# Strassen's seven products in the first feed-forward product of four chunks, on one Trainium2 core

## The chip, the core and the metric

The kernel runs on one core of a Trainium2 chip. The metric is the device time of one execution in microseconds. Before the change four runs gave 675.12, 676.35, 673.66 and 674.65 us; the median is 674.89. The core's engines have their own instruction queues and wait for each other by semaphores: PE multiplies matrices into PSUM, and its weight loads are listed apart as PEld; DVE (vector), ACT (scalar) and POOL (GpSimd) do elementwise work; SP issues most transfers. [...]

## What is computed

A linear attention (delta rule) over 4 batches, 8 heads, 768 tokens and head size 48 is followed by a feed-forward network with a leaky slope for each feature, on 3072 tokens:

```python
for t in range(S):
    kt, vt, bt = (k_n[:, :, t], v[:, :, t], beta[:, :, t, None])
    y[:, :, t] = np.einsum('bhd,bhde->bhe', q[:, :, t], state)
    v_old = np.einsum('bhde,bhd->bhe', state, kt)
    state = state + bt[:, :, :, None] * np.einsum('bhd,bhe->bhde', kt, vt - v_old)
...
h = x @ w_in                                  # 3072 x 384 by 384 x 2048
g = np.maximum(h, 0.0) + alpha * np.minimum(h, 0.0)
return (g @ w_out).astype(np.float32)         # 3072 x 2048 by 2048 x 384
```

Everything is float32. `x` is `y` with its heads side by side.

## The kernel before, in words

**Chunks and steps.** The sequence is cut into 12 chunks of 64 tokens. A chunk of all four batches has 256 tokens. The attention treats two batches at a time, so there are 24 steps `n`, two for each chunk, and every step depends on the state that the step two before it left. When both steps of a chunk `c` are done, `to_ffn` has transposed the chunk's output into `xts[c]`, three blocks of 128 model dimensions by 256 tokens, and the feed-forward of that chunk can run.

**First product, `ffn_in` (L894).** Features are taken in pairs of 128. For each pair, six matmuls (two feature blocks, three blocks of the contraction) of 256 columns fill one PSUM bank `p_ffn` (L903). ACT then takes Relu of the negated bank (L913), and DVE, once for each block of features, multiplies by the slope and adds the bank (L915). The result lies in `act`. There are eight pairs in a chunk. Two banks take turns.

**Second product, `ffn_out_fast` (L955).** From chunk 2 on this product already uses Strassen's scheme (Winograd's form): seven products of 192 columns, each over the eight pairs (L967), instead of eight. It needs sums of blocks of `act`, made by DVE in `operand_sums` (L848, L857), four for each half of the pairs, and sums of the weights, made once. DVE adds the seven products up (L987), and the rows are stored.

**The order of the work** is written out by hand; instructions stand on each engine's queue in program order. From step `JOINED` on, each step has three bursts of attention on PE: `burst_a` (L1070: the outputs and the next state of the step before, the reading of the state for this one), `turn_round` (L1101: transposes) and `burst_b` (L1090: the solve, Gram matrices, and two small products). Between them `stretch` (L1403) deals out a number of parts of the feed-forward, and with `weave` shares other pieces among them: elimination pieces on DVE (`blocks`), copies on ACT that place blocks (`placing`, L615) and what the burst returned as `later`. The feed-forward lags the attention by about one chunk; that of chunk 11 runs after the attention has ended.

**PSUM** has eight banks. Six are three pairs `p_big`, taken in turn by the bursts; two are the `p_ffn` banks.

**Names that the steps below touch:** the query is the product of `q` with the state in `through_state` (L735 to L739), copied to `y` by ACT (L755). `k_t` has nine rotating buffers, `same` and `block` one each (elimination), `k_early` three for keys that have been loaded ahead. The last elimination is that of steps 20 to 23.

Of the kernel before, what the change touches and what calls it, by code (L numbers as in the profile page):

```python
# [32 lines left out]
C = 64  # L33
# [2 lines left out]
BUSY = 8  # L36
EARLY = 8
FIRST = 6


@with_exitstack
def kernel(
# [26 lines left out]
    work = ctx.enter_context(tc.tile_pool(name="work", bufs=2))  # L69
    psum = ctx.enter_context(tc.tile_pool(name="psum", bufs=1, space=bass.MemoryType.PSUM))  # L70

    def ps_big():


        return psum.tile([128, 2, 512], FP32, name="p_big", tag="big", bufs=3)

    def ps_one():
        return ps_big()[:, 0]

    ffn_banks = [psum.tile([128, 512], FP32, name=f"p_ffn{i}") for i in range(2)]  # L80
    turn = [0]

    def ps_ffn():
# [3 lines left out]
    def half(i):  # L87
        return slice(64 * i, 64 * i + 64)

    def dims(i):  # L90
        return slice(64 * i, 64 * i + D)
# [224 lines left out]
    def by_parity(x):  # L316
        return x.rearrange("p (g a) d -> p a g d", a=2)
# [70 lines left out]
    def quarters():  # L388
        return [(g, a, t) for g in range(G) for a in range(2) for t in range(2)]

    def now(pieces):
        for x in pieces:
            x()

    def region(p, n, **into):

        p = ps_big()[:, :, 0:n] if p is None else p
        assert p.shape[-1] == n
        return p.rearrange("p a (g i) -> p a g i", **into)
# [310 lines left out]
        return [filled]  # L710


    nv, rhs_, ys, us, xts = {}, {}, {}, {}, {}

    def scale_v(n):
        if n < N and n not in nv:
            nv[n] = v_raw.pop(n)
            nc.vector.tensor_tensor(
                out=nv[n], in0=nv[n],
                in1=stats[n][0][:, :, None].to_broadcast([128, H, D]), op=ALU.mult,  # L720
            )

    def through_state(n, p=None, p_y=None):
        if n >= N:
            return []
        c, bp = steps[n]
        if c == 0:
            rhs_[n] = by_parity(nv[n])
            return []
        p = region(p, G * (D + C), g=G)  # L730
        for g, a, t in quarters():
            nc.tensor.matmul(  # L732
                p[half(t ^ a), a, g], k_t[n][dims(a), g, half(t)], beside[bp][dims(a), t, g]
            )
        p_y = region(p_y, G * D, g=G)  # L735
        for g, a, t in quarters():
            nc.tensor.matmul(  # L737
                p_y[half(t), a, g], q_t[n][dims(a), t, g], state[bp][dims(a), t, g]
            )  # L739

        r = work.tile([128, 2, G, D], FP32, name="r")
        v_in = by_parity(nv[n])
        y = work.tile([128, H, D], FP32, name="y")
        rhs_[n], ys[n] = r, y

        def less(to, own, a):
            nc.vector.tensor_tensor(  # L747
                out=r[to, a], in0=v_in[to, a], in1=p[own, a, :, 0:D], op=ALU.subtract
            )

        return [
            lambda: less(slice(0, 128), slice(0, 128), 0),
            lambda: less(half(0), half(1), 1),
            lambda: less(half(1), half(0), 1),
            lambda: nc.scalar.copy(by_parity(y), p_y),  # L755
            lambda: masked(n, p[:, :, :, D : D + C]),
        ]

# [48 lines left out]
    def to_ffn(n, p=None):  # L807
        c, bp = steps[n]
        if bp == 0:
            xts[c] = work.tile([128, KT, TOK], FP32, name="xt", tag="xt", bufs=NXT)  # L810
        p = (ps_one() if p is None else p)[:, 0:DM]
        y = ys[n].rearrange("p h d -> p (h d)")
        for t in range(KT):
            nc.tensor.transpose(p[:, t * 128 : (t + 1) * 128], y[:, t * 128 : (t + 1) * 128], ident)  # L814

        nc.scalar.copy(  # L816
            xts[c].rearrange("p k (u b t i) -> p b k u t i", u=2, b=NB, t=2)[:, bp],
            p.rearrange("p (k t u i) -> p k u t i", k=KT, t=2, u=2),
        )


    gss = {}
# [132 lines left out]
    def ffn_out_fast(c):  # L955
# [58 lines left out]
        store(c, 1, o[1])  # L1014
        yield

    in_done, out_done = [], []
    IN_PARTS, OUT_PARTS, FAST_PARTS = FT * KT, NB * FT, 7 * FP // 2


    def part(gen, n):
        for _ in range(n):
            next(gen, None)
            yield
# [45 lines left out]
    def burst_a(n):  # L1070

        soon, later = [], []
        b = ps_big()
        if n > JOINED:
            soon += outputs(n - 1, b[:, :, 0:WY])
            soon += next_state(n - 1, b[:, :, WY : 2 * WY])
            later.append(lambda: load_late(n + 1))
        if n < N:
            p, y = ps_big(), ps_big()
            soon += through_state(n, p[:, :, 0 : G * (D + C)], y[:, :, 0:WY])  # L1080
            if n < JOINED + 2:
                soon += between_1(n + 1, b[:, :, 2 * WY : 2 * WY + G * HB])
            if n == JOINED:
                soon += grams(n + EARLY, y[:, :, WY : WY + G * C])
                later.append(lambda: squares(n + EARLY + 1))
            later.append(lambda: load_v(n + 3))
        now(soon)
        return later

    def burst_b(n):  # L1090

        b, x = ps_big(), ps_big()[:, :, 0 : G * C]
        soon = solve(n, b[:, :, 0:WY])
        gram = grams(n + EARLY + 1, x)
        soon += between_2(n + 1, b[:, :, WY : WY + G * HB])
        if n > JOINED:
            soon += between_1(n + 2, b[:, :, 2 * WY : 2 * WY + G * HB])
        now(soon + gram[:2])
        return gram[2:] + [lambda: squares(n + EARLY + 2)]

    def turn_round(n):  # L1101
# [24 lines left out]

    def queries():

        p = [x.rearrange("p (n g i) -> p n g i", n=2, g=G) for x in ffn_banks]
        for n in range(2):  # L1130
            for g, a, t in quarters():
                nc.tensor.matmul(
                    p[a][half(t ^ a), n, g], k_t[n][dims(a), g, half(t)],
                    q_t[n][dims(a), t, g],
                )
            a_t[n] = work.tile([128, H, C], FP32, name="a_t")

        def mask(n):
            for a in range(2):
                nc.vector.tensor_tensor(  # L1140
                    out=a_t[n][:, a * G : (a + 1) * G], in0=p[a][:, n],
                    in1=minus[:, None, :].to_broadcast([128, G, C]), op=ALU.mult,
                )

        return mask
# [248 lines left out]
    weave((prelude(NJ), 4), (catch_up(), 2 * (EARLY - FIRST)), (part(late, few), few))  # L1394

    def feed_forward():
        for c in range(2, NCH):
            yield from ffn_in(c)
            yield from ffn_out_fast(c)

    tail = feed_forward()

    def stretch(n, blocks, share, later, *gens):  # L1403

        gens = [(*x, 0.0) for x in (*gens, (part(tail, n), n))]
        gens += [(part(blocks, share), share, 0.3), (each(later), len(later), 0.5)]
        weave(*[x for x in gens if x[1] > 0])

    blocks, share = eliminate(2), WHOLE // 3
# [9 lines left out]
    TURNS = [(3, 3, 4), (3, 3, 4), (4, 4, 4), (0, 5, 6)]  # L1419
    FILL = {JOINED: (8, 12, 12), JOINED + 1: (10, 12, 10), JOINED + 2: (8, 10, 12)}  # L1420
    FILLS = [(12, 10, 12), (12, 18, 12)]
    for n in range(JOINED, N):
        fill, share = FILL.get(n, FILLS[n % 2]), PIECES_OF.get(n, TURNS[n % NJ])
        extra = [[], [], []]
        if n == JOINED:
            place(n + 1, (0,))
            extra[1] = [(weight_sums(1, 0, 3), 3)]
            extra[2] = [(weight_sums(0, 3, 4), 1)]
        elif n == JOINED + 1:
            extra[0] = [(weight_sums(1, 3, 4), 1), (placing(n + 1, (1, 2, 3)), PLACING)]  # L1430

        later = burst_a(n)
        stretch(fill[0], blocks, share[0], later, *extra[0])
        later = turn_round(n)
        if n == JOINED:
            extra[1].append((placing(n + 1, (1, 2, 3)), PLACING))
        stretch(fill[1], blocks, share[1], later, *extra[1])
        m, ends = (n + 6) // NJ, n % NJ == 2
        if ends and n > JOINED:
            for _ in blocks:  # L1440
                assert False
            place(n + 2, (0,))
        later = burst_b(n) + [lambda: scale_v(n + 1)]
        if n == JOINED:
            stretch(fill[2], blocks, share[2], later, *extra[2])
            for _ in blocks:
                assert False
            place(n + 2, (0,))
            place(n + 3, (0,))
            blocks = eliminate(m)  # L1450
        else:
            if ends:
                blocks = eliminate(m) if m < N // NJ else iter(())
            after = [(placing(n + 2, (1, 2, 3)), PLACING)]
            if n % NJ != 1:
                after.append((placing(n + 3, (0,)), 1))
            stretch(fill[2], blocks, share[2], later, *after, *extra[2])
    stretch(12, iter(()), 0, burst_a(N))
    to_ffn(N - 1)
    for _ in tail:  # L1460
# [31 lines left out]
```

## Time and profile before

The profiled execution took 675.12 us; its span, from the first to the last instruction, is 673.4 us.

| what | us | share of the span |
|---|---|---|
| PE busy | 651.0 | 97% |
| PE, first product (L903), 1152 records | 261.6 | |
| DVE busy | 452.4 | 67% |
| ACT busy | 271.0 | 40% |
| POOL busy | 35.7 | 5% |
| first product of chunk 8 starts at | 489.74 | |
| first product of chunk 9 starts at | 538.36 | |
| first product of chunk 10 starts at | 586.17 | |
| first product of chunk 11 starts at | 630.60 | |
| second product of chunk 11 starts at | 651.32 | |

The page cuts the span into 40 slices and gives each engine's busy share in tenths:

```profile
PE   6999999999998999999999999999999999999997
...
DVE  4956879868989869748959748759655355354261
ACT  4927755336565353353353353243244144020110
POOL 6000121001010000001000000000000000000000
```

Each digit is one slice of 16.8 us, 9 being 90% or more. A float32 matmul is listed as two records with a weight load each, so the 48 matmuls of one chunk's first product are 96 records. [...]

### The profile page before, as it was taken

How to read it: one execution, taken by the hardware profiler on the slowest of the kernel's cores; microseconds unless marked ns; L12 is line 12 of the kernel's file. 1: busy time of each engine (PE TensorE's matmuls, PEld its weight loads, DVE VectorE, ACT ScalarE, POOL GpSimd, SP SyncE). 2: the span in 40 equal slices, each digit the busy share in tenths (PEclk: the TensorE clock that was granted, in tenths of full speed). 3: DMA queues.
4: the chain of work that ended last, by engine and by line, in shares of the span. 5: the costliest groups of instructions: out<-in, count | busy, mean ns of one | idle time of the engine just before them, and what ended most of it. 6: DMA issues, size and time to landing. Idle time of an engine off the chain costs nothing.

```text
span 673.4 us, 21591 instructions
## 1 busy us (share of the span) xinstructions
PE 651.0 (97%) x9359; PEld 567.4 (84%) x9359; DVE 452.4 (67%) x1125; ACT 271.0 (40%) x643; POOL 35.7 (5%) x105
## 2 busy tenths in 40 slices
PE   6999999999998999999999999999999999999997
PEld 5578877666687998998998998988989989989997
DVE  4956879868989869748959748759655355354261
ACT  4927755336565353353353353243244144020110
POOL 6000121001010000001000000000000000000000
PEclk9979999999999999999999999999999999999999
DMA  8837844211432022122112111111111110100000
GB/s 130 235 94 209 208 107 118 71 37 30 80 61 49 17 58 48 25 50 49 25 38 37 26 37 37 26 42 31 28 44 27 37 37 2 37 1 2 23 1 24
DMA packets 110959, 37.69 MB, mean 56 GB/s; under 512 B 104160, under 2 KB 107248, under 8 KB 110864
## 3 DMA queue, kind: packets, MB, share of 16 engines
q1 hardware_dynamic: 109088, 35.81, 24.3%
q8 instruction: 74, 1.21, 0.7%
q10 hardware_dynamic: 1776, 0.49, 0.4%
q14 instruction: 21, 0.17, 0.1%
HBM read 31.56 MB, written 4.72 MB: 54 GB/s over the span
## 4 chain that ended last, share of the span: by engine, by line
PE 77%; DVE 14%; ACT 6%; issue 2%; DMA 1%; ACTq 0%; POOL 0%; SPq 0%; DVEq 0%; POOLq 0%
PE p_ffn L903 30%; PE p_ffn L967 28%; DVE prod L499 2%; PE p_big L360 2%; DVE block L505 2%; PE p_big L762 2%; PE p_big L732 2%; PE p_big L775 2%; PE p_big L407 2%; DVE act L915 2%; PE p_big L1121 2%; ACT diag L631 1%; PE p_big L737 1%; PE p_big L791 1%; DMA ke<-in_k_dram 1%
## 5 line engine op out<-in xcount | busy, mean ns | idle before, releaser
L903 PE MATMUL p_ffn<-xt,w_in 128*128 128x256 f32 x1152 | 261.6, 382 | 6.0 <-ACT act L913 1.8
L903 PEld LDWEIGHTS p_ffn<-xt,w_in 128*128 128x128 f32 x1152 | 214.4, 190 | 37.7 <-issue 3.1
L915 DVE SCALAR_TENSOR_TENSOR act<-act,al_t,p_ffn 128x256 f32<-128x256 f32 x176 | 76.6, 477 | 79.6 <-ACT act L913 79.5
L913 ACT ACTIVATE act<-p_ffn 128x512 f32<-128x512 f32 x88 | 52.4, 595 | 143.0 <-PE p_ffn L903 142.7
L967 PE MATMUL p_ffn<-w_out,act 128*128 128x192 f32 x480 | 82.5, 328 | 0.2 <-DVE act L915 0.2
L967 PEld LDWEIGHTS p_ffn<-w_out,act 128*128 128x128 f32 x480 | 77.6, 190 | 1.0 <-issue 0.5
L505 DVE TENSOR_TENSOR block<-block,prod 128x30 f32<-128x30 f32 (+9 forms) x150 | 49.9, 333 | 5.1
L499 DVE TENSOR_TENSOR prod<-block 128x30 f32<-128x30 f32 (+9 forms) x150 | 48.9, 326 | 3.3 <-POOL block L489 1.6
L987 DVE TENSOR_TENSOR o_sb<-u,p_ffn 128x192 f32<-128x192 f32 x40 | 13.3, 352 | 50.3 <-PE p_ffn L967 41.9
L816 ACT COPY xt<-p_big 128x384 f32<-128x384 f32 x22 | 10.4, 477 | 74.2 <-PE p_big L814 74.2
L967 PE MATMUL p_ffn<-space_out,sums 128*128 128x192 f32 x160 | 29.4, 327 | 0.0
L967 PE MATMUL p_ffn<-more,sums 128*128 128x192 f32 x160 | 29.3, 326 | 0.0
L755 ACT COPY y<-p_big 128x384 f32<-128x384 f32 x22 | 10.4, 476 | 43.0 <-PE p_big L737 41.4
L967 PE MATMUL p_ffn<-w_out,sums 128*128 128x192 f32 x160 | 27.6, 326 | 0.0
L967 PEld LDWEIGHTS p_ffn<-more,sums 128*128 128x128 f32 x160 | 26.6, 190 | 0.0
L967 PEld LDWEIGHTS p_ffn<-space_out,sums 128*128 128x128 f32 x160 | 26.5, 190 | 0.1
L967 PEld LDWEIGHTS p_ffn<-w_out,sums 128*128 128x128 f32 x160 | 26.3, 190 | 0.0
L708 ACT COPY inv<-p_big 32x256 f32<-32x256 f32 x38 | 13.8, 362 | 29.7 <-DVE u L766 29.4
L631 ACT ACTIVATE diag<-inverse,which 64x128 f32<-64x128 f32 (+2 forms) x60 | 24.3, 405 | 2.4 <-DVE inverse L472 1.4
L747 DVE TENSOR_TENSOR r<-v_raw,p_big 64x192 f32<-64x192 f32 (+1 forms) x66 | 23.2, 352 | 1.0
L332 DVE TENSOR_REDUCE norm<-ksq 128x8 f32<-128x384 f32 x24 | 13.0, 545 | 13.5 <-ACT ksq L330 13.5
L349 POOL TENSOR_TENSOR beta_t<-beta_t,rec 128x8 f32<-128x8 f32 x24 | 6.2, 260 | 291.6 <-DVE rec L347 271.3
(161 smaller groups left out, 954.2 us busy)
## 6 DMA issues: line engine op xcount, KB each, us to landing
w_out<-in_moe_w_in_dram SPq DMA_DIRECT2D x12, 512.0 KB, 5.6
qp<-in_q_dram SPq DMA_DIRECT2D x48, 96.0 KB, 3.0
v_raw<-in_v_dram SPq DMA_DIRECT2D x48, 96.0 KB, 2.8
kl<-in_k_dram SPq DMA_DIRECT2D x96, 48.0 KB, 2.5
out_dram<-o_sb SPq DMA_DIRECT2D x92, 48.0 KB, 1.6
space_out<-in_moe_w_out_dram SPq DMA_DIRECT2D x11, 384.0 KB, 3.9
ke<-in_k_dram SPq DMA_DIRECT2D x43, 96.0 KB, 3.1
w_out<-in_moe_w_out_dram SPq DMA_DIRECT2D x5, 384.0 KB, 4.6
```

The lines of the kernel that those rows point to most:

```text
L360: nc.tensor.transpose(p[0:ROWS, g * 128 : (g + 1) * 128], src[:, 2 * g : 2 * g + 2].rearrange("p h d -> p (h d)")[:, 0:ROWS], ident,)
L407: nc.tensor.matmul(p[half(t), a, g], k_t[n][dims(a), g, half(t)], k_t[n][dims(a), g, half(t)])
L499: nc.vector.tensor_tensor(out=prod, in0=r[:, 0:j, j : j + 1].to_broadcast([128, j, n]), in1=r[:, j : j + 1, j + 1 : HB].to_broadcast([128, ...
L505: nc.vector.tensor_tensor(out=r[:, 0:j, j + 1 : HB], in0=r[:, 0:j, j + 1 : HB], in1=prod, op=ALU.add)
L631: nc.scalar.mul(out, x, which[rows, i : i + 1])
L708: nc.scalar.copy(to[rows], p[rows])
L732: nc.tensor.matmul(p[half(t ^ a), a, g], k_t[n][dims(a), g, half(t)], beside[bp][dims(a), t, g])
L747: nc.vector.tensor_tensor(out=r[to, a], in0=v_in[to, a], in1=p[own, a, :, 0:D], op=ALU.subtract)
L903: nc.tensor.matmul(p_h[:, i], w_in[:, t, (f + i) * 128 : (f + i + 1) * 128], xt[:, t], start=(t == 0), stop=(t == KT - 1),)
L913: nc.scalar.activation(g, p_h, ACT.Relu, scale=-1.0)
L915: nc.vector.scalar_tensor_tensor(out=g[:, i], in0=g[:, i], scalar=al_t[:, f + i : f + i + 1], in1=p_h[:, i], op0=ALU.mult, op1=ALU.add,)
L967: nc.tensor.matmul(p, x(i), w(i), start=(i == 0), stop=(i == FP - 1))
```

## The change

In chunks 8 to 11 (`FAST_IN = 8`) the first product of each feature pair is made anew. The first two blocks of the contraction, the two blocks of features and the two halves of the tokens make two-by-two blocks of 128; they are multiplied by Strassen's seven products (Winograd's form) of 128 columns. The third block of the contraction stays as it was: two matmuls of 256 columns into the same bank. So a pair has 2 matmuls of 256 columns and 7 of 128, instead of 6 of 256.

Three of the seven products go straight into the pair's bank; four go into a bank of their own (`shared`), which ACT copies to SBUF; POOL forms three running sums there, and DVE adds the result to the pair's bank (`total`). Relu (`below`) and slope then work on SBUF. `Due` puts these pieces at counted places later in the order: the total one pair on, Relu and slope two pairs on, except for the last pairs. Relu has two buffers, and the last total and slope are put ahead of most operand sums.

The sums of the weights (`input_sums`, eight on DVE) are made once, beside the second product of chunk 7; they lie in `same`, in buffers of early keys, in a `k_t` buffer and, in place, in `w_in`. The sums of the tokens (`token_sums`, four on DVE) are made for each chunk during the second product of the chunk before.

From step 16 on PSUM is divided into two pairs for the attention instead of three, and four banks for the feed-forward. The query moves from `burst_a` of a step to `burst_b` of the step before. Copies that `burst_b` left for later are shared out from an earlier point (`soon=0.1`), and `placing` is put off to the stretch after the next `burst_a`. In chunks 8 to 11 `ffn_out_faster` replaces `ffn_out_fast`: the same seven products in another order, with the last two pairs of the first two products held back, and the store of the second half of the rows first.

```diff
-        return psum.tile([128, 2, 512], FP32, name="p_big", tag="big", bufs=3)
+        big.append(big.pop(0))
+        return big[-1]
...
+    banks(3, 0)
...
+    def query(n, p=None):
...
+        for g, a, t in quarters():
+            nc.tensor.matmul(
+                p[half(t), a, g], q_t[n][dims(a), t, g], state[bp][dims(a), t, g]
+            )
+        ys[n] = work.tile([128, H, D], FP32, name="y")
+        return [lambda: nc.scalar.copy(by_parity(ys[n]), p)]
...
+            for dst, x, y, op in (
+                (s1, a21, a22, ALU.add), (s2, s1, a11, ALU.subtract),
+                (s3, a11, a21, ALU.subtract), (a21, a12, s2, ALU.subtract),
+            ):
+                nc.vector.tensor_tensor(out=dst, in0=x, in1=y, op=op)
+                yield
...
+        for dst, a, b in (
+            (0, x(0, 1), x(0, 0)), (1, x(1, 1), t[:, 0]), (2, x(1, 1), x(0, 1)),
+            (3, x(1, 0), t[:, 1]),
+        ):
+            nc.vector.tensor_tensor(out=t[:, dst], in0=a, in1=b, op=ALU.subtract)
...
+    def ffn_in_fast(c):
...
+            p = ffn_banks[i % 3]
+            q = quarter(ffn_banks[2 if i == 0 else 3])
...
+            def own():
+                whole(0)
+                yield
+                more(0, w(1, 0), x(1, 0))
+                more(1, w(0, 1), x(1, 1))
+                yield
+                whole(1)
+                yield
+                more(2, w(1, 1), t[:, 3])
+                yield
+
+            def common():
+                shared(0, w(0, 0), x(0, 0))
+                shared(1, s(1), t[:, 1])
+                yield
+                shared(2, s(2), t[:, 2])
+                shared(3, s(0), t[:, 0])
+                nc.scalar.copy(z, q)
+                for dst, a, b in (
+                    (z[:, 1], z[:, 0], z[:, 1]), (z[:, 2], z[:, 1], z[:, 2]),
+                    (z[:, 1::2], z[:, 1:3], z[:, 3:4].to_broadcast([128, 2, 128])),
+                ):
+                    nc.gpsimd.tensor_tensor(out=dst, in0=a, in1=b, op=ALU.add)
+                yield
+
+            def total():
...
+                nc.vector.tensor_tensor(
+                    out=h, in0=p, in1=z.rearrange("p i e -> p (i e)"), op=ALU.add
+                )
+
+            def below():
...
+                nc.scalar.activation(r.rearrange("p f i -> p (f i)"), h, ACT.Relu, scale=-1.0)
+
+            def slope():
+                for f in range(2):
+                    nc.vector.scalar_tensor_tensor(
+                        out=g[:, f], in0=r[:, f], scalar=al_t[:, 2 * i + f : 2 * i + f + 1],
+                        in1=g[:, f], op0=ALU.mult, op1=ALU.add,
+                    )
+
+            due.put(PER * (i + 1) + {0: PER, FP - 1: 2}.get(i, 3), total)
+            due.put(PER * (i + 2) + {FP - 2: 1, FP - 1: -4}.get(i, 2), below)
+            due.put(PER * (i + 2) + {FP - 2: 1, FP - 1: -2}.get(i, 5), slope)
+            for gen in (own(), common()) if i == 0 else (common(), own()):
+                for _ in gen:
+                    due.step()
+                    yield
...
+    def ffn_out_faster(c):
...
+        yield from some(*a, range(FP - 2))
+        yield from some(*b, range(FP - 2))
+        yield from some(*a, range(FP - 2, FP))
+        nc.scalar.copy(u[0], p[0])
+        yield from some(*b, range(FP - 2, FP))
+        add(o[0][:, left], u[0], p[1])
+        yield from some(p[2], operand(1, 1), w_sum_(3), range(FP))
...
+        asked = query(n + 1, x[:, :, 0:WY]) if n + 1 >= LATE else []
...
+        if n >= LATE:
+            now(soon[:1])
+            return soon[1:] + asked
...
+        if n == LATE:
+            banks(2, 2)
...
-        stretch(fill[0], blocks, share[0], later, *extra[0])
+        stretch(fill[0], blocks, share[0], later, *extra[0], *put_off)
```

## The prediction

> **What bounds the kernel now.** I read the page's first part, then sums over windows, then waits, then the timeline.
>
> ```profile
> PE 651.0 (97%) x9359; PEld 567.4 (84%) x9359; DVE 452.4 (67%) x1125; ACT 271.0 (40%) x643; POOL 35.7 (5%) x105
> ```
>
> PE is busy for 97% of the span, but an average hides stages. The changed stretch runs from the feed-forward of chunk 8 (489.74 us) to the last matmul. Three of its windows (chunk 8 with two attention steps; first product of chunk 11; its second product):
>
> ```profile
> 489.74:538.36 48.62, 48.40 (x672) 44.37 (x671) 24.54 (x52) 17.02 (x40) 0.00 (x0) 1.00 0.17 34
> 630.60:651.32 20.72, 20.72 (x98) 18.24 (x97) 8.96 (x19) 4.18 (x7) 0.00 (x0) 1.00 0.04 12
> 651.32:669.50 18.18, 18.18 (x113) 18.07 (x111) 5.49 (x12) 0.92 (x2) 0.00 (x0) 1.00 0.05 12
> ```
>
> The columns are length, then busy PE, PEld, DVE, ACT, POOL, then clock. PE has no gap, DVE is half used, POOL is empty, the clock is full. The waits of PE from 488 us to the end agree:
>
> ```profile
> PE p_big L665 <- ACT diag L631: 0.2, 1, 0.2
> ```
>
> So every PE nanosecond removed here shortens the run, as long as the new ACT, POOL and DVE work keeps up. After the last matmul an addition (0.35) and the store take 4 us; both versions end so.
>
> **PE, removed and added.** An f32 matmul leaves two records. The first product of chunk 11 is 96 records in 20.72 us: 215.8 ns each at 256 columns. One pair of feature blocks has 12 records, 2.590 us. Afterwards it has 4 records of 256 columns and 14 of 128 (seven 128-column products). What does a 128-column record cost, each with its own weight load?
>
> ```profile
> 555.21 0.49 PE L814 MATMUL p_big<-ident,y 128*128 128x128 f32 x3
> 555.53 0.60 PE L360 MATMUL p_big<-ident,qp 128*112 128x128 f32 x4
> 555.97 0.38 PE L903 MATMUL p_ffn<-xt,w_in 128*128 128x256 f32 x1
> ...
> 555.86 0.30 PEld L903 LDWEIGHTS p_ffn<-xt,w_in 128*128 128x128 f32 x2
> ```
>
> From 555.21 to 555.97 stand seven records: 109 ns each. These are transposes, with a weight load of 140 ns on the PEld side where the product's takes 190. But the first load for L903 begins at 555.86 and its matmul at 555.97: the load of the very shape in question, begun with the transpose before, holds nothing up within one 109 ns slot. At 36.1 us one ordinary f32 matmul of 128 columns (L1121) shows 109 ns between its two records too, with a 190 ns load between.
>
> [...] The row has single f32 loads only, never a long stream; still it shows the load of this very shape inside the slot, so I take 109.2. Break-even is 109.2 + 198/14 = 123.3 ns. Below nothing there is no end: fewer columns can't gain more than their share.
>
> Four chunks of eight pairs: 32 x 0.198 = **6.3 us** removed. Going from 128 to 256 columns costs 3 ns (the record after 555.97 came after 219 instead of 216), twice a pair: 0.2 back.
>
> **New work beside PE, per pair of 2.39 us.** ACT: a PSUM copy of 128x512 (nearest row: L381, 112x512, 582 ns) and Relu from SBUF (L913, 595): 1.2, before 0.6. DVE: the total of 128x512, one operand in PSUM (L427, 692) and two slopes (0.87 for the two of L915): 1.56, before 0.87. POOL: two additions of 128x128 and one of 128x256, in place and one after the other. No row has them. Nearest:
>
> ```profile
> L456 POOL COPY same<-right 32x256 f32<-32x256 f32 x18 | 8.2, 457 | 32.5 <-DVE right L413 22.5 <-DVE rec L347 9.6
> L350 POOL TENSOR_TENSOR wgt<-beta_t,rec 128x8 f32<-128x8 f32 x24 | 6.9, 286 | 1.9
> ```
>
> Undisturbed, L350 takes 204 and L456 390: 0.76 ns per element for one input. Low end 293 + 293 + 390 = 0.98 us. [...] So each engine alone fits into 2.39. Together they may not, since POOL and DVE can exclude each other:
>
> ```profile
> 215.77 1.27 POOL L489 TENSOR_SCALAR_AFFINE_SELECT block<-block 128x1024 f32<-128x1024 f32 x1 [17.83 <-DVE block L472]
> ...
> 216.31 1.25 DVE L857 TENSOR_TENSOR sums<-act,sums 128x512 f32<-128x512 f32 x1
> ```
>
> L857 takes 0.69 elsewhere; here it ended 0.53 after POOL did. The new slopes read two SBUF tensors, as L857 does; the old ones had one in PSUM and show no such delay. Laid out for one pair from the start of its shared products: they end on PE at 0.87, the ACT copy runs 1.1 to 1.7, POOL 1.75 to 3.5, or to 3.85 with one slope between its additions; the total then ends at 4.6. (The additions need the copy. The total needs them and the pair's own products, which end at 2.39 + 0.2; slope 1 before it waits for Relu, which stands behind the copy on ACT and ends at 2.3.) The same term buffer is written again two pairs on, at 4.78 + 1.1 = 5.9. Slack 1.3 us. The bank of the shared products is copied out at 1.7 and wanted at 2.39: slack 0.7. In this steady state PE doesn't wait. The change adds one dangerous wait: ACT's copy for pair i + 2 stands until DVE has made total i. Behind it on ACT are Relu i, the attention's copies and, through the bank, PE's shared products of pair i + 3.
>
> Where it may wait:
> - A burst of attention hands DVE 3.4 us at once (549.63 to 553.03 in the trace), ahead of the next total. In chunk 8, with B the start of the burst after pair 2: slope 0, held up by Relu 0 and two POOL additions, ends at B + 1.8, the burst's DVE work at B + 5.2, total 2 at B + 5.9 (0.69). The copy for pair 4 wants it at B + 1.64 (the burst on PE, without the query) + 2.39 + 1.1 = B + 5.1. It is 0.8 late, the bank has 0.7 in hand, so PE stands for 0.1 us, and for 0.5 if one more POOL addition falls into a slope; I take 0.3. Chunks 8, 9 and 10 have such a burst in their first product: 0.9. That the last total and slope go ahead of the operand sums keeps those sums (0.69 each, both inputs in SBUF) out of this chain; with them ahead it would be up to 2.1 us longer.
> - The end of a first product. In chunk 11, T being its last matmul: the copy for pair 7 ends at T - 0.7, Relu 5 at T - 0.1, slope 5 at T + 1.2, slope 6 at T + 2.15, total 7 at T + 2.85, Relu 7 at T + 3.45, slope 7 at T + 3.95 and 4.4. The second product runs its first two sums over pairs 0 to 5 before, 24 records at 162.5 (18.18 us over 112) = 3.9 us, and wants slope 7 at T + 4.2 and 4.55. Just in time; 0.3 for error. The operand sums (7 x 0.69) end near T + 9.9 and the product over the last batch of s2 begins at T + 9.1, needing the fifth of them, ready at T + 7.9.
> - Chunk 7's second product gets eight input sums on DVE (shape of L857, 0.69: 5.5 us) and four token sums (0.29 each by L505's 128x130): 20 us of DVE work in about 21. The token sums end some 1.7 us before the fifth product of chunk 8 asks for them: 0.
>
> **Moved without price.** The query's 16 matmuls (L737, 0.56 us) go from one burst to the other. The blocks put off to the next burst are 3.3 us of ACT in a stretch of 4.8 that also holds 2.4 of new work; their deadline is a burst later, and the copy for pair 4 is then at most 0.1 late, inside its 0.7. PSUM pairs drop from three to two: by the same layout the last readers of a pair end 1.1 us before the next burst. SP issues the same stores, two groups swapped; no load is added.
>
> **Sum.** -6.3 + 0.2 + 0.9 + 0.3 = -4.9. The profiled execution took 675.12, so 670.2; the median of the runs, 674.89, lies 0.2 lower, so 670.0.
>
> **Rivals.**
> 1. *Weight loads set the pace of 128 columns* (slower). [...] Against: the loads in 109 ns slots. [...] It decides from 123.3 ns a record. Chance 0.12.
> 2. *POOL and DVE take turns throughout.* [...] For: the 1.25 us row. Against: POOL's first addition overlaps the total, which reads PSUM. Chance 0.17, from 672 to 676.5.
> 3. *Gain not delivered*, because the start of chunk 8 stalls for the buffers that it borrows (old keys, blocks): 675. Against: elimination ends before, by its shares. Chance 0.03.
>
> **Numbers.** My forecast 0.68, own range 668.3 (all 6.3 and 0.3 of scatter) to 672. Range 668.3 to 675.5: it leaves out rival 1 and rival 2's end. What tells from no change is 0.3%, 2.0 us: faster below 672.9: 0.68 + 0.05 of rival 2 = 0.73; same 0.09 + 0.03 = 0.12; slower 0.12 + 0.03 = 0.15.
>
> **What would show it.** Right: 128-column records start 109 ns apart; a pair takes 2.39 us; from chunk 8's first product to the last matmul 174.9 us instead of 179.8; PE waits under 2 us in all there. Wrong: record spacing over 123 ns; PE waiting for the ACT copy in every pair; POOL additions above 0.6 and 0.9 us; PE waits over 4 us.

## The result and the profile after

After the change the median of 33 runs is 669.27 us (665.67 to 677.64), that of 54 runs of the kernel before 674.73. The ratio is 0.992, with a 95% interval of 0.9903 to 0.9937: faster by 5.5 us, with 4.3 to 6.5 as the interval. The profiled execution took 668.09 us, with a span of 666.4.

From the page of after, the busy times and three rows of slices:

```profile
PE 643.2 (97%) x9551; PEld 567.5 (85%) x9551; DVE 493.2 (74%) x1181; ACT 288.1 (43%) x675; POOL 92.7 (14%) x201
...
DVE  4965889878989869748949747859869658568383
...
POOL 6000121001010000001000000000035044052260
PEclk9999999999999999999999999999999999999999
```

PE has 192 records more (6 a pair) and is busy 7.8 us less, still 97% of the span. DVE went from 67% to 74%. POOL, empty in the second half before, has four humps now: the four first products. The clock row of before reads

```profile
PEclk9979999999999999999999999999999999999999
```

with a 7 in its third slice, before all that is changed. The two profiled executions differ by 7.0 us, and 0.92 of it lies ahead of chunk 7. So the profiles are compared from there on, by the start of each chunk's first product, and not by their spans:

| | chunk 7 | 8 | 9 | 10 | 11, to the last matmul | sum |
|---|---|---|---|---|---|---|
| before | 48.88 | 48.62 | 47.81 | 44.43 | 38.76 | 228.50 |
| after | 48.27 | 46.96 | 46.52 | 43.13 | 37.53 | 222.41 |
| difference | -0.61 | -1.66 | -1.29 | -1.30 | -1.23 | -6.09 |

Windows of after that answer to the three of before (length, busy PE, PEld, DVE, ACT, POOL, clock):

```profile
488.21:535.16 46.95, 46.95 (x719) 45.04 (x719) 33.78 (x64) 21.05 (x48) 13.95 (x24) 1.00 0.20 38
624.82:644.23 19.41, 19.41 (x146) 18.59 (x145) 11.59 (x20) 7.87 (x14) 13.48 (x23) 1.00 0.05 14
644.23:662.50 18.27, 18.27 (x114) 18.04 (x112) 10.03 (x21) 1.58 (x3) 1.15 (x2) 1.00 0.05 12
```

PE is busy for the whole of each. The first product of chunk 11 takes 19.41 us instead of 20.72, with POOL busy for 13.5 of them, and the second product takes 0.09 us longer. The waits of PE from 480 us to the end: the list of after is empty. One loss is too short for that list. In the second product of chunk 11 two weight loads that otherwise follow each other every 0.162 us start 0.30 apart:

```profile
648.13 0.19 PEld L1246 LDWEIGHTS p_more<-w_out,act 128*128 128x128 f32 x1
...
648.43 0.19 PEld L1246 LDWEIGHTS p_more<-w_out,act 128*128 128x128 f32 x1
```

The second load reads a block of `act` whose slope DVE finished at 648.38. PE loses 0.08 us: its records start at 648.455 and 648.700, which is 0.245 apart instead of 0.162. So the new work costs PE next to nothing.

How fast do the records come? PE's timeline in chunk 11 over one pair (start, time from the first record's start to the last one's end, the group):

```profile
634.52 0.39 PE L1161 MATMUL p_more<-xt,w_in 128*128 128x128 f32 x2
...
635.41 0.60 PE L1151 MATMUL p_ffn<-xt,w_in 128*128 128x256 f32 x2
...
635.85 0.61 PE L1156 MATMUL p_ffn<-xt,w_in 128*128 128x128 f32 x4
...
636.29 0.60 PE L1151 MATMUL p_ffn<-xt,w_in 128*128 128x256 f32 x2
...
636.73 0.38 PE L1156 MATMUL p_ffn<-k_t,w_in 128*128 128x128 f32 x2
...
636.95 0.39 PE L1161 MATMUL p_more<-xt,w_in 128*128 128x128 f32 x2
```

Records overlap (a record of 256 columns lasts 379 ns and the next follows 216 after its start), so only starts are to be read: 634.52 to 635.41 are the eight records of the shared products, 111.6 ns each; two of 256 columns take 434 and four of 128 columns 444; the next two groups repeat this with two records of 128 columns at the end, and the pair ends at 636.95, after 2.43 us. The forecast had 2.392.

POOL's additions and DVE's slopes from chunk 8 on, grouped by shape (busy, mean ns | idle before, releaser):

```profile
L1185 POOL TENSOR_TENSOR k_t<-k_t 128x128 f32<-128x128 f32 x32 | 17.1, 535 | 165.3 <-ACT k_t L1180 164.1
L1185 POOL TENSOR_TENSOR block<-block 128x128 f32<-128x128 f32 x32 | 15.1, 473 | 15.2 <-ACT block L1180 13.9
L1185 POOL TENSOR_TENSOR k_t<-k_t 128x256 f32<-128x256 f32 x16 | 12.4, 774 | 1.3
...
L1200 DVE SCALAR_TENSOR_TENSOR act<-k_t,al_t,act 128x256 f32<-128x256 f32 x32 | 21.1, 700 | 0.1
L1200 DVE SCALAR_TENSOR_TENSOR act<-block,al_t,act 128x256 f32<-128x256 f32 x32 | 19.7, 657 | 5.1 <-ACT block L1196 5.1
```

The additions of 128x128 take 473 and 535 ns on average, those of 128x256 take 774; the shortest of 128x128 takes 452. The slopes are stretched: 0.66 to 0.70 each on average, where two in a row without an addition beside them take 0.87. POOL's large idle time stands before the pairs' copies, so POOL waits for work and not the other way round.

### The profile page after: what moved, and what is told of

The parts are those of the page before. It is cut to its first block, busy times and chain, and to the rows that moved or that the text cites. A ratio compares the mean times of both kernels' runs of the same rounds, so it can differ in the third digit from the quotient of the medians.

```text
span 666.4 us, 22184 instructions
## 1 busy us (share of the span) xinstructions
PE 643.2 (97%) x9551; PEld 567.5 (85%) x9551; DVE 493.2 (74%) x1181; ACT 288.1 (43%) x675; POOL 92.7 (14%) x201
## 3 DMA queue, kind: packets, MB, share of 16 engines
q8 instruction: 75, 1.23, 0.8%
## 4 chain that ended last, share of the span: by engine, by line
PE 76%; DVE 15%; ACT 6%; issue 2%; DMA 1%; ACTq 0%; POOL 0%; DVEq 0%; POOLq 0%
PE p_ffn L993 17%; PE p_ffn L929 16%; PE p_more L1246 8%; PE p_more L1161 4%; PE p_ffn L1151 3%; PE p_ffn L1246 3%; PE p_ffn L1156 2%; PE p_pair L377 2%; DVE prod L516 2%; DVE block L522 2%; PE p_pair L786 2%; PE p_pair L424 2%; DVE act L941 2%; PE p_pair L761 2%; PE p_pair L799 2%
## 5 line engine op out<-in xcount | busy, mean ns | idle before, releaser
L929 PE MATMUL p_ffn<-xt,w_in 128*128 128x256 f32 x768 | 175.4, 383 | 5.0 <-ACT sums L939 1.8
L929 PEld LDWEIGHTS p_ffn<-xt,w_in 128*128 128x128 f32 x768 | 142.4, 190 | 26.3 <-ACT sums L939 2.2
L941 DVE SCALAR_TENSOR_TENSOR act<-act,al_t,p_ffn 128x256 f32<-128x256 f32 x112 | 48.6, 475 | 28.7 <-ACT act L939 28.6
L1185 POOL TENSOR_TENSOR k_t<-k_t 128x128 f32<-128x128 f32 (+1 forms) x48 | 29.5, 614 | 166.6 <-ACT k_t L1180 164.1
L993 PE MATMUL p_ffn<-w_out,act 128*128 128x192 f32 x288 | 49.6, 328 | 0.2 <-DVE act L941 0.2
L993 PEld LDWEIGHTS p_ffn<-w_out,act 128*128 128x128 f32 x288 | 46.5, 190 | 0.8 <-issue 0.5
L1185 POOL TENSOR_TENSOR block<-block 128x128 f32<-128x128 f32 (+1 forms) x48 | 27.6, 575 | 16.4 <-ACT block L1180 13.9
L1151 PE MATMUL p_ffn<-xt,w_in 128*128 128x256 f32 x96 | 28.7, 380 | 0.0
L771 DVE TENSOR_TENSOR r<-v_raw,p_pair 64x192 f32<-64x192 f32 (+1 forms) x66 | 23.2, 352 | 1.1
L1200 DVE SCALAR_TENSOR_TENSOR act<-block,al_t,act 128x256 f32<-128x256 f32 x32 | 19.7, 657 | 5.1 <-ACT block L1196 5.1
L1246 PE MATMUL p_more<-w_out,act 128*128 128x192 f32 x128 | 21.9, 329 | 0.0
```

What stands on the lines that cost most here:

```text
L771: nc.vector.tensor_tensor(out=r[to, a], in0=v_in[to, a], in1=p[own, a, :, 0:D], op=ALU.subtract)
L929: nc.tensor.matmul(p_h[:, i], w_in[:, t, (f + i) * 128 : (f + i + 1) * 128], xt[:, t], start=(t == 0), stop=(t == KT - 1),)
L941: nc.vector.scalar_tensor_tensor(out=g[:, i], in0=g[:, i], scalar=al_t[:, f + i : f + i + 1], in1=p_h[:, i], op0=ALU.mult, op1=ALU.add,)
L993: nc.tensor.matmul(p, x(i), w(i), start=(i == 0), stop=(i == FP - 1))
L1151: nc.tensor.matmul(p[:, f * 256 : f * 256 + 256], w(2, f), xt[:, 2], start=True, stop=False)
L1185: nc.gpsimd.tensor_tensor(out=dst, in0=a, in1=b, op=ALU.add)
```

## The experiments

All lengths below are taken as in the table above; the clock there is 1.00 in every one of them.

| kernel | median, us | ratio to before | chunk 7 | 8 | 9 | 10 | 11 | sum |
|---|---|---|---|---|---|---|---|---|
| e1_plain_first | 682.55 | 1.0073 [1.0038, 1.0109] | 48.27 | 48.27 | 47.84 | 45.56 | 40.74 | 230.68 |
| e1b_plain_first | 673.98 | 0.9975 [0.9945, 1.0006] | 48.27 | 48.27 | 47.84 | 44.45 | 38.75 | 227.59 |
| e4_from_chunk_10 | 674.13 | 0.9964 [0.9935, 0.9994] | 48.27 | 48.27 | 47.84 | 43.13 | 37.54 | 225.05 |
| e2_adds_on_dve | 674.97 | 0.9972 [0.9943, 1.0001] | 48.27 | 47.51 | 47.46 | 44.58 | 39.07 | 226.89 |
| e3_pool_twice | 680.11 | 1.0066 [1.0033, 1.01] | 48.27 | 47.89 | 47.45 | 45.75 | 44.12 | 233.49 |
| e6_one_relu_buffer | 670.03 | 0.9912 [0.9879, 0.9945] | 48.27 | 46.96 | 46.52 | 43.27 | 38.39 | 223.41 |
| e7_sums_ahead | 673.41 | 0.9964 [0.9926, 1.0002] | 48.27 | 47.90 | 47.46 | 44.68 | 39.33 | 227.64 |
| e8_query_moved | 676.5 (one run) | | 49.60 | 48.30 | 47.84 | 44.45 | 38.76 | 228.94 |
| e9_copies_put_off | 675.57 (one run) | | 48.24 | 48.62 | 47.81 | 44.43 | 38.76 | 227.86 |
| e10_before_again | 673.77 (one run) | | 48.88 | 48.62 | 47.80 | 44.43 | 38.76 | 228.50 |
| e11_placing_alone | 675.7 (one run) | | 48.24 | 48.62 | 47.80 | 44.43 | 38.76 | 227.86 |

The chunks agree to a few hundredths wherever a kernel's order is the same, while runs of one kernel differ by several microseconds. So effects of 1 us are read from the chunks, and only the larger ones from the times. Most of that scatter lies ahead of chunk 7, which begins between 437.6 and 447.8 us in these profiles. In e1 it begins at 446.5, 5.6 us later than in before, so e1's median is 6.6 us above that of before while its chunks hold 2.2.

**Is it Strassen's columns, or the new order and the banks?** In e1 the first product is made as before, six matmuls of 256 columns; the new banks, the order and the second product stay.

```diff
-            p = ffn_banks[i % 3]
+            p = ffn_banks[i % 4]
...
+                for f in range(2):
+                    for k in range(KT):
+                        nc.tensor.matmul(
+                            p[:, f * 256 : f * 256 + 256], w(k, f), xt[:, k],
+                            start=(k == 0), stop=(k == KT - 1),
+                        )
+                        yield
...
-            due.put(PER * (i + 1) + {0: PER, FP - 1: 2}.get(i, 3), total)
...
+            due.put(PER * (i + 1), below, slope)
```

> Everything of the change except Strassen in the first product: four feed-forward banks, two pairs for the attention, the query in the other burst, the second product's new order stay; chunks 8 to 11 use six matmuls of 256 columns again, without input sums, token sums, copies and additions. Theory (the gain is the PE columns removed, nothing else): as before, ratio 0.998 to 1.002, a pair 2.59 us. Rival (the new order and the banks bring the gain): ratio 0.996 or less.

It is 1.1 and 2.0 us too long in chunks 10 and 11, which no theory had. Its waits of PE name the reason:

```profile
PE p_more L1217 <- DVE act L1174: 2.8, 2, 1.7
```

Pair 7 lay in the fourth bank, which the second product writes first, so PE stood until pair 7's slope had read it. That is a fault of this edit, not of the order that it was to test. e1b keeps `ffn_banks[i % 3]` as the change does:

> As the run with the plain first product, but its pairs go through banks 0 to 2 in turn, so that the last pair no longer lies in the bank that the second product writes first (PE waited 2.8 us for it there). Theory: no wait of PE; from chunk 8's first product to the last matmul 179.3 us (before 179.6, after the change 174.1); ratio 0.998 to 1.001. Rival (order and banks bring the gain): 175 us, ratio 0.994 or less.

No wait of PE is left in it. From before to e1b the sum falls by 0.91 us, from e1b to after by 5.18. The columns make 5.18 / 32 = 0.162 us a pair, or 0.164 without the 0.08 us lost at 648.4. The times agree: the intervals of e1b and after do not overlap. e4 uses Strassen's scheme in chunks 10 and 11 alone (`FAST_IN = 10`):

> Strassen's first product in chunks 10 and 11 only; the rest of the change as it is. Theory (1.3 to 1.4 us for each chunk): half the gain, ratio 0.9945 to 0.9975. Rival (a fixed gain of the new order, or a fixed cost at the first such chunk): ratio near 0.992, or 0.999 and above.

Chunks 8 and 9 are those of e1b, chunks 10 and 11 those of after: each chunk brings its own share (1.32 us, and 1.23 in chunk 11 with its 0.08 of loss), and none depends on the one before.

**What sets the pace of a 128-column record?** Streams of equal matmuls are put behind the kernel's end, each matmul with its own weight load and nothing to wait for:

```diff
+    stream(8, ws, xs[:, 0:256])
+    stream(16, ws, xs[:, 0:128])
+    stream(8, ws, xs[:, 0:192])
+    stream(16, ws, xs[:, 0:64])
+    stream(8, ws, xs[:, 0:160])
+    stream(16, ws[:, 0:64], xs[:, 0:128])
+    stream(8, ws, xs[:, 0:256])
+    stream(32, narrow[:, 0:128], narrow[:, 128:256])
```

> After the last product PE runs streams of equal matmuls, each with its own weight load: f32 of 256, 128, 192, 64, 160 moving columns with 128 weight columns, 128 moving columns with 64 weight columns, and bf16 with 128 by 128; results unused. Theory (a record's pace is the longer of its columns and its weight load): 216, 112, 162.5, 112, 136 ns, with 64 weight columns 109, all start to start. [...]

From start to start of the records, inside each stream:

```
float32, 256 columns, 128 weight columns   216 ns
float32, 192 columns                       162.5
float32, 160 columns                       136
float32, 128 columns                       111.7
float32,  64 columns                       111.7
float32, 128 columns,  64 weight columns   109.2
bfloat16, 128 columns, 128 weight columns   55.8
```

Two records 28 apart of the stream with 64 columns, and two 28 apart of the stream with 64 weight columns, give these paces from their starts (3.13 and 3.06 us):

```profile
669.96 0.39 PE L1758 MATMUL p_ffn<-xt,w_in 128*128 128x64 f32 x2
...
673.09 0.39 PE L1758 MATMUL p_ffn<-xt,w_in 128*128 128x64 f32 x2
...
675.90 0.38 PE L1758 MATMUL p_ffn<-xt,w_in 128*64 128x128 f32 x2
...
678.96 0.38 PE L1758 MATMUL p_ffn<-xt,w_in 128*64 128x128 f32 x2
```

64 columns are no faster than 128, so here something else than the columns sets the pace. With half the weight columns the pace is 109.2 ns, and the line through 256 and 192 columns gives 109.1 at 128. So the floor of 111.7 ns, 2.6 above that line, goes with the weight columns. The weight load is the likely cause; that it is the load, and not something else that grows with the weight columns, is not shown. Float32 at 128 columns loses 2.5 ns against the 109.2 of the forecast, whose break-even lay 14.1 ns higher, at 123.3. The bfloat16 stream runs at 55.8 ns, half of the 111.7.

**How much room have POOL and DVE?** e2 puts the three additions on DVE.

```diff
-                    nc.gpsimd.tensor_tensor(out=dst, in0=a, in1=b, op=ALU.add)
+                    nc.vector.tensor_tensor(out=dst, in0=a, in1=b, op=ALU.add)
...
+            due.put(PER * i + (PER + 4 if i == 0 else PER), sums_of)
```

> The three additions of a pair go from POOL to DVE, after the pair's own products. Theory (DVE has no room for them: 0.69 total + 0.87 slopes + 1.0 additions = 2.56 us against 2.43 of PE, and a burst's 3.4 us on top): PE waits 2 to 6 us in all, ratio 0.995 to 1.001. Rival (POOL and DVE excluding each other is what costs, the additions themselves fit): no wait of PE, ratio 0.992 or less, slopes at 0.87 us for two throughout.

The sum is 4.5 us longer than that of after. DVE's timeline in its chunk 11:

```profile
643.58 1.07 DVE L1188 TENSOR_TENSOR k_t<-k_t 128x128 f32<-128x128 f32 x3
644.75 0.69 DVE L1192 TENSOR_TENSOR act<-p_more,k_t 128x512 f32<-128x512 f32 x1
645.36 0.87 DVE L1202 SCALAR_TENSOR_TENSOR act<-block,al_t,act 128x256 f32<-128x256 f32 x2
646.15 1.07 DVE L1188 TENSOR_TENSOR block<-block 128x128 f32<-128x128 f32 x3
```

With POOL silent two slopes take 0.87 again, and the three additions 1.07, less than the 1.79 of POOL's in after where no slope runs beside them (491.50 us). But DVE has 2.57 us of work for each pair of 2.43, and falls behind: PE waits 3.3 us for slopes at the start of second products, as the theory had it. POOL is slower for the job and still the right place.

e3 doubles each addition on a tile that nobody else uses.

```diff
+                    nc.gpsimd.tensor_tensor(
+                        out=filler[:, 0:n], in0=filler[:, 0:n], in1=filler[:, 0:n], op=ALU.mult
+                    )
```

> After each of the three additions POOL makes one more of the same size on a spare tile, so its work is doubled; nothing reads it. Theory (POOL with 2.15 of 2.43 us is hidden but nearly full): POOL sets the pace, some 4.0 us a pair; 8 x 1.6 us a chunk less the 2.5 to 3.5 us that bursts give in chunks 8 to 10: about +40 us, 700 to 718 us. Rival (POOL is far from the path, its busy time is stretched by waiting): under 674 us.

It costs 11.1 us on the sum, far less than the 40 or so that were expected. PE's waits from 480 us on, and two records of its timeline, one pair apart:

```profile
PE p_more L1251 <- DVE act L1205: 6.3, 6, 1.6
PE p_more L1162 <- ACT k_t L1181: 1.0, 2, 0.5
PE p_more L1251 <- ACT block L1181: 0.5, 1, 0.5
PE p_more L1162 <- ACT block L1181: 0.5, 1, 0.5
```

```profile
640.42 0.49 PE L1162 MATMUL p_more<-xt,w_in 128*128 128x128 f32 x2
...
643.60 0.49 PE L1162 MATMUL p_more<-xt,w_in 128*128 128x128 f32 x2 [0.49 <-ACT k_t L1181]
```

In the last pairs of chunk 11 the chain that the forecast named comes true (L1162): PE waits for the ACT copy, which waits for the term buffer, and a pair takes 3.18 us, the pace of POOL. Most of the waiting (L1251, 6.8 of 8.3 us) stands at the start of the second products, where the slopes come late. The added operations were shorter than assumed (0.40 and 0.61 us). Chunks 8 and 9 pay 0.9 us each, chunk 10 pays 2.6 and chunk 11 pays 6.6; even there the first pairs still follow each other after 2.43 us. So the expectation's price was wrong twice: the operation's, and that every pair would pay it.

**The two buffers and the late sums.** e6 gives Relu one buffer:

```diff
-            r = held["less"] if i % 2 == 0 else quarter(held["block"][:, 512:1024])
+            r = held["less"]
```

> Relu of every pair goes to one buffer instead of two. Theory (only the end of a first product is tight): Relu 6 must wait for slope 5, slope 7 comes 0.7 us later, PE waits about 0.6 us in chunk 11, as much or less in chunk 10, nothing in 8 and 9: +0.5 to 1.3 us, ratio 0.992 to 0.995. Rival (the buffer decides in every pair): PE waits in each chunk, over 4 us in all, ratio 0.998 or more.

```profile
PE p_more L1246 <- DVE act L1200: 0.7, 1, 0.7
```

One new wait in chunk 11, and 1.0 us on the sum (0.14 in chunk 10, 0.86 in chunk 11), as the theory had it; the times of the two kernels can't tell them apart. e7 puts three of the operand sums ahead of the last total and slope:

```diff
-        for at in (6, 6, 7, 7, 8, 9, 10):
+        for at in (2, 2, 2, 7, 8, 9, 10):
```

> Three operand sums (batch 0) stand ahead of the last total and slope on DVE again. Theory: slope 7 is 3 x 0.61 = 1.8 us later; in chunk 11 PE, which had 0.1 us in hand, waits 1.8 us, in chunk 10 about 1.2, in 8 and 9 next to nothing, since a burst of 1.8 us lies between: +3 us, ratio 0.995 to 0.998. Rival (DVE catches up before PE needs it): no wait, ratio 0.992.

```profile
PE p_more L1246 <- DVE act L1200: 4.2, 4, 1.6
```

DVE's timeline at the end of its chunk 11:

```profile
657.73 0.68 DVE L883 TENSOR_TENSOR act<-act 128x512 f32<-128x512 f32 x1
658.33 0.68 DVE L883 TENSOR_TENSOR sums<-act,sums 128x512 f32<-128x512 f32 x1
658.93 0.68 DVE L1190 TENSOR_TENSOR act<-p_ffn,block 128x512 f32<-128x512 f32 x1
660.37 0.88 DVE L1200 SCALAR_TENSOR_TENSOR act<-block,al_t,act 128x256 f32<-128x256 f32 x2 [0.76 <-ACT block L1196]
```

The total stands behind the sums, Relu behind the total, and slope 7 begins 5.5 us after the last matmul of the first product (654.90 us) instead of 3.7. All four chunks wait, also 8 and 9, where next to nothing was expected: the sum is 5.2 us longer, as much as Strassen's columns bring. Without the ordering of the change the columns would bring nothing.

**Where do the other 0.9 us come from?** Before has two short waits of PE from chunk 7 on, which neither after nor any of e1 to e7 shows:

```profile
PE p_ffn L903 <- ACT xt L816: 0.3, 1, 0.3
PE p_big L665 <- ACT diag L631: 0.2, 1, 0.2
```

The first lies in chunk 7 (0.45 us between the starts of two records beyond the usual distance, and 0.19 more behind it), the second in chunk 8. e8 is the kernel before with only the query moved from step 16 on; e9 is before with only the copies of `burst_b` shared out earlier and `placing` put off.

```diff
+        asked = query(n + 1, x[:, :, 0:WY]) if n + 1 >= LATE else []
...
-        now(soon + gram[:2])
+        now(soon + asked + gram[:2])
```

> The kernel before with one part of the change: from step 16 on the query runs in burst_b of the step before. Three PSUM pairs, the copies and the placing stay as before, no Strassen in the first product. The trace of before has two PE waits that no kernel with the change shows: 0.64 us in chunk 7 (0.45 and 0.19 late around the first L903 after the transposes, put down to the copy of xt on ACT) and 0.22 in chunk 8 (L665 for diag). Theory A: the query's move takes away the first (its ACT copy and 0.56 us of PE leave burst_a, the copy of xt or the slope that frees the bank comes earlier against PE): chunk 7 takes 48.27 us instead of 48.88, and chunk 8 stays at 48.6. Theory B: two pairs instead of three and the new order of banks did it, not the query: chunk 7 stays at 48.88. Theory C: those waits were one execution's scatter: a kernel that keeps this part as before may show 48.3 as well, which the next run tells apart.

```diff
+        if n >= 16:
+            now(soon[:1])
+            return soon[1:]
...
+            if n >= 16:
+                put_off, after = after, []
```

> The kernel before with another part of the change alone: from step 16 on the copies of burst_b are shared out from an earlier point and placing goes to the stretch after the next burst_a; the query stays in burst_a, three PSUM pairs, no Strassen in the first product. Theory A: chunk 7 stays at 48.88 us (its waits come from the query in burst_a), and the 0.22 us wait of L665 for diag in chunk 8 goes (48.4 instead of 48.62), since the diag copies come earlier. Theory C (scatter of one execution): chunk 7 at 48.3 here too. If placing that is put off comes too late for the elimination, a new wait of DVE or PE shows in chunk 8 or 9, longer than 48.62 and 47.81.

Theory A had it the wrong way round, and theory B falls. The query's move takes away chunk 8's wait (48.30), and in chunk 7 it puts a longer one in place of the old (49.60):

```profile
PE p_ffn L912 <- DVE act L924: 1.0, 1, 1.0
```

e9 clears chunk 7 (48.24) and leaves chunk 8's wait of 0.2 us where it was (48.62). In e1b, which has both parts and more, the two chunks take 48.27 each; no run has the two parts alone. Is chunk 7's wait the scatter of one execution (theory C), and which of e9's two edits clears it? e10 is before unchanged; e11 puts off `placing` and leaves the copies of `burst_b` alone.

> The kernel before once more, unchanged, for a second profile. If its two waits belong to its order, chunk 7 takes 48.88 us again (within 0.03) and chunk 8 48.62. If chunk 7's 0.64 us was one execution's scatter, chunk 7 takes about 48.25.

> The kernel before with only placing put off to the stretch after the next burst_a from step 16 on; burst_b's copies are shared out from where they were. If the placing blocks on ACT and DVE caused chunk 7's wait, chunk 7 takes 48.24 us as with both edits; if the copies of burst_b and their earlier point did it, 48.88. Chunk 8 should stay at 48.62 in either case, with the 0.22 us wait for diag.

Before shows both waits again, with the same chunks to 0.01 us, so theory C falls; and e11 has all of e9's effect. It is the putting off of `placing`. With it DVE's work in chunk 7 comes earlier: the masking of `a_t` (L427) starts 14.6 us after the chunk's first product in e9 and e11, and 15.7 in before, while PE comes to the transposes (L814) 16.84 us after it in e9 and in before. So PE finds done what it waited for. The profile names the copy of `xt` on ACT (ended 458.87 us in before), but the slope on DVE that frees a bank ended only just before it (458.77). The traces tell them apart. In e11 PE goes on to L903 while that copy is still running:

```profile
459.64 0.47 ACT L816 COPY xt<-p_big 128x384 f32<-128x384 f32 x1
...
459.71 0.81 PE L903 MATMUL p_ffn<-xt,w_in 128*128 128x256 f32 x3
```

The slope had ended there at 458.88. In e8 the copy ends at 459.83, and PE starts only at 460.56, after the slope's end at 460.42. So PE waited for the slope, and the releaser that the profile names in before is the wrong one. Two pairs of PSUM instead of three are not needed for either effect.

## Why the prediction was right

The forecast was 670.0 us; the median came to 669.27. The likeliest case happened, by its mechanism: fewer columns on PE, which bounds the kernel, with nearly everything new hidden beside it. That the number came so close is in part luck, since three terms were off and offset each other. By its steps:

- **A pair's gain, forecast 0.198 us, measured 0.162.** The forecast took 2.590 less 4 x 215.8 + 14 x 109.2 = 2.392 us. The gain is 0.164 without the 0.08 us lost at the end of chunk 11. The term that was mis-sized is the 128-column record: 109.2 ns, from transposes, against 111.7 in the product. Twelve of a pair's fourteen records take 2.5 ns more, 0.030 us; the other two, the first of each run of 128 columns, do come after 109 ns, which is why the single load behind a transpose could not show it. The two steps from 128 to 256 columns cost 0.005, as the forecast had in its 0.2 us. Rival 1, weight loads that set the pace, was to decide from 123.3 ns; of the 14.1 ns up to there the streams of e5 show 2.5, and that the load causes them is not shown. The columns bring 5.2 us, not 6.3 less 0.2.
- **Waits, forecast 1.2 us, measured 0.08.** The layout was close. In chunk 11's steady state:

```profile
634.52 0.39 PE L1161 MATMUL p_more<-xt,w_in 128*128 128x128 f32 x2
...
635.66 0.59 ACT L1180 COPY k_t<-p_more 128x512 f32<-128x512 f32 x1 [1.36 <-PE p_more L1161]
...
636.32 2.15 POOL L1185 TENSOR_TENSOR k_t<-k_t 128x128 f32<-128x128 f32 x3 [0.32 <-ACT k_t L1180]
...
638.51 0.69 DVE L1190 TENSOR_TENSOR act<-p_ffn,k_t 128x512 f32<-128x512 f32 x1 [0.62 <-POOL k_t L1185]
```

  From the pair's start to the end of its total are 4.7 us, forecast 4.6; POOL's chain takes 2.15, with a slope falling into it, forecast 2.1. No run shows the term of 1.75 us that the layout gives the three additions without a slope (1.75 to 3.5); what after shows is 1.79 (491.50 us). The burst of chunk 8 delays total 2 to 503.05 us and the copy for pair 4 by 0.2, not 0.8, which the bank's 0.7 covers. At the end of chunk 11, where the forecast said "just in time" and charged 0.3, DVE's timeline shows slope 7:

```profile
644.21 1.53 DVE L1200 SCALAR_TENSOR_TENSOR act<-block,al_t,act 128x256 f32<-128x256 f32 x2
645.67 0.87 DVE L1200 SCALAR_TENSOR_TENSOR act<-k_t,al_t,act 128x256 f32<-128x256 f32 x2
646.46 0.68 DVE L1190 TENSOR_TENSOR act<-p_ffn,block 128x512 f32<-128x512 f32 x1
647.90 0.88 DVE L1200 SCALAR_TENSOR_TENSOR act<-block,al_t,act 128x256 f32<-128x256 f32 x2 [0.76 <-ACT block L1196]
```

  The first product ends at 644.23. Slope 7 ends at 648.38 for the first block of features, 4.15 us later, where the forecast had 3.95; PE's load for it comes 0.14 us late, and PE loses 0.08. So there is no slack left at this place, which is why e6 and e7 pay at once.
- **The steps "moved without price" had one, a gain of 0.9 us.** The wait of L665 for diag stood in the forecast's own view and wasn't followed up, and its window didn't begin early enough to hold chunk 7's. e11 and e8 share it out: putting off `placing` brings 0.64 in chunk 7, the query's move 0.32 in chunk 8; the query's move alone costs 0.7 in chunk 7.
- **Rival 2 (POOL and DVE take turns)** is half true: a slope that meets an addition is stretched (1.53 us for two instead of 0.87), as in the table of groups. It did not decide, since an addition meets a slope for part of its time only and the pair's 2.43 us of PE still cover both. Single additions of 128x128 reach 0.82 us (641.71 us), beyond the 0.6 that the forecast called a sign of being wrong; their means, 0.47 and 0.54, stay below it. No run shows the two taking turns throughout, and the range that goes with the rival's chance, 672 to 676.5, was the author's estimate. **Rival 3** did not happen: chunk 8 starts without a wait.

The errors by size: the columns brought 0.9 us less than forecast (5.2 for 6.1), the waits cost 1.1 us less, and the order brought 0.9 more. The sum from chunk 7 on is -6.1 for a forecast of -4.9; the medians differ by 5.5, with 4.3 to 6.5 as the interval, so the runs hold both. From the start of chunk 8's first product to the start of the last matmul the time went from 179.6 to 174.1 us, 5.5 less, where the forecast had 4.9 less (179.8 to 174.9, measured to 0.1 us behind that start).

## What to carry to other kernels

Where one engine is busy without a gap, take work off it at the price of the other engines' slack, and count that slack for each unit of the loop (here 2.43 us, with DVE at 1.56 to 2.2 and POOL at 2.15), and once more at the seam to the next stage, where the order of a few instructions on DVE is worth as much as the columns bring. Take the pace of a new shape from a run of that shape: a record of another operation was 2% off, which was about a sixth of the gain. A wait of 0.2 us that the profile lists is part of what a reordering can win or lose, and the releaser that the profile names need not be its cause: here a second trace in which the order differs told the two candidates apart.

## What the runs showed of the hardware

- In long streams a float32 record with 128 weight columns came every 111.7 ns, at 64 moving columns as at 128 (e5). So a float32 product with 128 weight columns gained nothing here from 64 columns instead of 128.
- The load records of these streams last 190 to 192 ns at a pace of 111.7 ns, so they overlap one another in the listing; the length of a load record is not its pace.
- In after, DVE and POOL held each other up where both read SBUF. In chunk 11 an addition that began at 634.388, 0.05 us after a slope, took 0.747 us instead of 0.456 and ended 0.31 after that slope; the next slope, begun during it, took 0.679 instead of some 0.475 and ended 0.28 after the addition. The totals, with one operand in PSUM, keep their 0.68 to 0.69: the one at 633.71 took 0.68 with an addition beside it from 633.85, and that addition 0.459.
